# Attention and MLP on one core: the first k rows staged in the second x's place, its k bands copied by GpSimd, a new order of work

## The chip, the cores and the metric

The kernel runs on one core of a Trainium2 chip. The metric is the device time of one execution in microseconds (us); smaller is better. The engines work in parallel, each through its own list of instructions in a fixed order: TensorE (PE in the profile; its weight loads are PEld), VectorE (DVE), ScalarE (ACT), GpSimd (POOL) and SyncE (SP), which here issues all transfers between HBM and the on-chip memory SBUF. TensorE writes its results to PSUM.

## The reference

```python
# q, k, v: (4, 8, 768, 64) float32; w_in: (512, 2048); w_out: (2048, 512)
block, window = (32, 16)
k_sum = k.reshape(B, H, nb, block, D).max(axis=3)
v_sum = v.reshape(B, H, nb, block, D).mean(axis=3)
mask_l = np.abs(pos[:, None] - pos[None, :]) < window
scores_l = scale * np.matmul(q, k.transpose(0, 1, 3, 2))         # kept where mask_l
scores_s = scale * np.einsum('bhsd,bhnd->bhsn', q, k_sum) + np.log(block)
a = softmax(concatenate([where(mask_l, scores_l, -1e9), scores_s]))
attn = np.matmul(a, concatenate([v, v_sum], axis=2))
x = attn.transpose(0, 2, 1, 3).reshape(B * S, H * D)             # (3072, 512)
h = x @ w_in
out = np.maximum(0.01 * h, h) @ w_out
```

Each row attends to a band of 31 neighbours and to 24 block summaries (the maxima of k and the means of v over 32 rows), and an MLP with a leaky ReLU follows.

## The kernel before

The 3072 rows of x are worked on in 8 chunks of 384 rows, two for each batch. Attention makes x of a chunk, transposed, in 12 units: 4 pairs of heads (p) by 3 tiles of 128 rows. Per unit TensorE computes scores (`s`, L329), VectorE adds the mask and finds the extreme (L334), ScalarE takes the exponential (L341), VectorE normalises (L378 to L386), TensorE transposes the weights (`t`, L346), ScalarE copies them to SBUF (`pt`), TensorE multiplies them with v (`o`, L352), and x is stored as a high part (`xhi`, ScalarE) and the rest (`xlo`, VectorE), so that two reduced-precision matmuls and a third with the low half of the weights give nearly full precision.

The MLP of a chunk has 16 blocks f of 128 hidden columns. Per block twelve matmuls make `h` (L676: win_hi times x high, win_hi times x low, win_lo times x high, for 4 contraction parts); ScalarE makes `ghi` and `gs`, VectorE the low part `glo`; nine matmuls of 512 columns add to the outputs `a` (L695 to L697). The weights are loaded once and split into high and low halves by ScalarE and VectorE (L631 to L644) while chunks 0 and 1 run. The parts are: chunk 0 with blocks 0 to 9, all of chunk 1, chunk 0 with blocks 10 to 15, then chunk after chunk.

k comes as a window of 800 columns per pair of heads (`kn`); from it VectorE takes the maxima (`ksum`, L207), and ScalarE copies two bands of 3x96 columns per pair into the operand tile `k` that also holds q (L274); VectorE adds the maxima there (L289). The means of v of the first batch are made by six matmuls on TensorE (`vps`, L243, blocks `vb` of v), copied to SBUF by ScalarE (L248), and spread into the v tiles by GpSimd (L285).

The order of work is not written by hand. `Plan` gets every operation with an engine, an assumed cost, a priority and its needs, and lists them in the order in which they would run by these costs; the numbers at the head of the file (`PLACE`, `WS`, `XP`, `OFF`, `LOADS` and others) are priorities. Every engine then runs its list in that order. Where the plan leaves TensorE idle in the opening, matmuls on zeros (`spare`, L788) are put in. Buffers are rings: `big` has 6 buffers for k, v blocks and raw weights, `k` has 2, `v` 3, `pt` 2, `out` 3.

Of the kernel before, what the change touches and what calls it, by code (L numbers as in the profile page):

```python
# [23 lines left out]
LK = 120  # L24
# [25 lines left out]
KS = -4  # L50
XW = 1
B1 = 6
USQ = 1.424
WT = 1.15
# [92 lines left out]
def POOL(n):  # L147
    return 130 + 1.0 * n


def build(tc, ctx, a):
# [42 lines left out]
    def gate(b):  # L194
        return k_op[CPB * b - 1, 1] if b else []


    kn_op = {}

    def k_max(b, p, t, ahead):  # L200
        def load():
            x = new("big", ("kn", b * CPB, p), [128, 1024], bufs=BIG)
            nc.sync.dma_start(out=x[:, :S + 2 * WIN], in_=a["k"][b, p])

        def red():
            x = tl["kn", b * CPB, p][:, WIN:WIN + S].rearrange("p (n r) -> p n r", r=BLK)
            nc.vector.tensor_reduce(out=new("ksum", ("ksum", b, p), [128, NS], bufs=5), in_=x, axis=AX.X, op=ALU.max)  # L207
        key = ("kn", b * CPB, p)
        kn_op[key] = load_op(key, t - 1.3 - ahead, load, after=gate(b), alloc=[("big", key, BIG)], size=128 * (S + 2 * WIN) * 4)
        ksum_op[b, p] = P.op("DVE", DVE(S), t, red, after=[kn_op[key]], use=[key], alloc=[("ksum", ("ksum", b, p), 5)])  # L210
# [23 lines left out]
    def v_mean_pe(t):  # L234
        def load(j):
            x = new("big", ("vb", 0, j), [128, 1024], bufs=BIG)
            nc.sync.dma_start(out=x.rearrange("p (t d) -> p t d", t=2), in_=a["v0"][j])

        def mm(j, i):
            if i + j == 0:  # L240
                new("a1", ("vps",), [128, 512], src=ps_acc, bufs=1)
            n = 2 * j + i
            nc.tensor.matmul(tl["vps",][:NS], mask[:, 3 * LK + 20 - 4 * n:3 * LK + 44 - 4 * n], tl["vb", 0, j][:, 512 * i:512 * i + 512],  # L243
                             start=n == 0, stop=n == 5)

        def copy():
            tl["vsum", 0] = new("out", ("vs0",), [128, 512], bufs=TPC)[:NS]
            nc.scalar.copy(tl["vsum", 0], tl["vps",][:NS])  # L248
        prev = [mask_op]
        for j in range(3):  # L250
            o = load_op(("vb", 0, j), t - 4.5 + 0.1 * j, lambda j=j: load(j), alloc=[("big", ("vb", 0, j), BIG)], size=128 * 4096)
            for i in range(2):
                prev = [P.op("PE", 856, t, lambda i=i, j=j: mm(j, i), after=[o] + prev, use=[("vb", 0, j), ("vps",)],
                             alloc=[("a1", ("vps",), 1)] if i + j == 0 else [])]
        vsum_op[0] = P.op("ACT", ACT(512, True), t + 0.1, copy, after=prev, use=[("vps",)], alloc=[("out", ("vsum", 0), TPC)])


    def operands(c, p, t, ahead):
# [33 lines left out]
        if cb:  # L292
            kn_op[kw] = load_op(kw, t - 1.3 - ahead, load_k, alloc=[("big", kw, BIG)], size=128 * (T + 2 * WIN) * 4)
        ks = [P.op("ACT", ACT(TPC * 96), t - 0.6 + (0 if b else XW), lambda j=j: windows(j), after=[lq, kn_op[kw]], use=[kk, kw]) for j in range(2)]
        lv = load_op(("v", c, p), t - 0.6 - ahead, load_v, alloc=[("v", kv, VR)], size=96 * TPC * 1024)
# [63 lines left out]
    def unit(u):  # L359
# [59 lines left out]
        o = P.op("PE", 216, v + 1.2 + off("tr"), tr, after=[nm], use=[("e", m)], alloc=[("a0", kt, 1)])  # L419
        o = P.op("ACT", ACT(256, True), v + 1.3 + off("pt"), pt, after=[o] + pt_of.get(m, []), use=[kt, ("pt", m)] if u % 2 else [kt], alloc=[] if u % 2 else [("pt", ("pt", m), PTR)])  # L420
# [36 lines left out]
    def pair(m):  # L457
# [55 lines left out]
        al = [(f"x{XB[c]}", ("x", c), 1)] if r == 0 else []  # L513
        o1 = P.op("ACT", ACT(256, True), v2 + 0.3, xhi, after=[o] + ([x_op[c][0]] if r else []), use=[("s0", go), ("x", c)], alloc=al)
        o2 = P.op("DVE", DVE(256), v2 + 0.35 - XP, xlo, after=[o1], use=[("s0", go), ("x", c)])
# [28 lines left out]
    def quad(q):  # L544
# [16 lines left out]

        def xhi():
            nc.scalar.copy(x_of(xh, c, r, 512), tl["s0", kb1])
# [4 lines left out]
        o = burst(ka, pa, "s", 1280, qk, after=[y for x in ps for y in k_op[c, x]], use=kk)  # L568
        pts = []
        for m, kt, vt in ((ms[0], kb, pb), (ms[1], ka1, pa1)):  # L570
# [30 lines left out]
            nm = P.op("DVE", DVE(4 * LK), pa + 0.45 + d, nrm, after=[rc], use=[("e", m), ("z", m)])  # L601
            ot = burst(kt, vt, "t", 510, tr, after=[nm], use=[("e", m)])
            pts.append(P.op("ACT", ACT(512, True), vt + 0.2, pt, after=[ot], use=[("to", kt)], alloc=[("pt", ("pt", m), PTR)]))
        o = burst(kb1, pb1, "o", 1340, av, after=pts + [y for x in ps for y in v_op[c, x]], use=[("pt", m) for m in ms] + kv)
        al = [(f"x{XB[c]}", ("x", c), 1)] if r == 0 else []
        o1 = P.op("ACT", ACT(512, True), pb1 + 0.2, xhi, after=[o] + ([x_op[c][0]] if r else []), use=[("s0", kb1), ("x", c)], alloc=al)
        o2 = P.op("DVE", DVE(512), pb1 + 0.25 - XP, xlo, after=[o1], use=[("s0", kb1), ("x", c)])
# [234 lines left out]
```

## Time and profile before

| | before |
|---|---|
| device time, median of 3 runs | 641.48 us (640.58 to 642.33) |
| the profiled execution's own time | 640.98 us |
| its span, first to last instruction | 639.2 us |
| busy: PE, PEld | 633.7 us (99%), 557.6 us (87%) |
| busy: DVE, ACT, POOL | 263.4 us (41%), 293.2 us (46%), 4.4 us (1%) |
| mean granted TensorE clock | 0.999 |

All stretches are counted in us from the span's start. Busy time of TensorE is modelled from the starts of its pipelined matmuls, so two neighbouring rows can overlap a little; the distance between two starts tells what a step took.

### The profile page before, as it was taken

Reading aid. Unit: us, or ns where it says so; the run is one execution under the profiler, and the core shown is the slowest. Engines: PE = TensorE matmul, PEld = TensorE weight load, DVE = VectorE, ACT = ScalarE, POOL = GpSimd, SP = SyncE. Lnnn points to the kernel's source line nnn. Section 1 sums busy time; section 2 is a strip of 40 time slices with the busy share of each in tenths; the row PEclk is TensorE's granted clock in tenths of the full one; section 3 lists DMA queues with packets and bytes.
Section 4 is the critical chain, followed back from the end, with each engine's and each line's share of the span. In section 5 each row is a group of like instructions: output and inputs, shape, how many; then the busy total and the mean of one; then the engine's idle time right before and its main releaser. Section 6 shows DMA issues by size and latency. Waiting matters only on the chain.

```text
span 639.2 us, 11599 instructions
## 1 busy us (share of the span) xinstructions
PE 633.7 (99%) x4592; PEld 557.6 (87%) x4592; DVE 263.4 (41%) x881; ACT 293.2 (46%) x876; POOL 4.4 (1%) x10
## 2 busy tenths in 40 slices
PE   9999999999999999999999999999999999999997
PEld 7688888898888998888888888888898898989996
DVE  5899999512485213323533243132332422121111
ACT  5899985624655224435345254243543532222221
POOL 0200000000000000000000000000000000000000
PEclk9999999999999999999999999999999999999999
DMA  8897997200754100304332121111101200010001
GB/s 272 275 303 240 295 296 219 75 4 26 199 157 126 40 2 14 122 24 125 87 86 72 42 68 33 47 63 32 41 13 47 86 1 1 1 50 0 1 1 50
DMA packets 27206, 58.07 MB, mean 91 GB/s; under 512 B 3024, under 2 KB 13328, under 8 KB 27152
## 3 DMA queue, kind: packets, MB, share of 16 engines
q1 hardware_dynamic: 27152, 57.33, 29.3%
q8 instruction: 36, 0.59, 0.4%
q14 instruction: 18, 0.15, 0.1%
HBM read 48.97 MB, written 6.29 MB: 86 GB/s over the span
## 4 chain that ended last, share of the span: by engine, by line
PE 99%; ACT 0%; issue 0%; DVE 0%
PE h L676 42%; PE a L695 14%; PE a L697 14%; PE a L696 14%; PE spare L788 2%; PE vps L243 1%; PE t L346 1%; PE o L352 1%; PE s L329 1%; PE s_('B', 21)_5358 L352 0%; PE s_('B', 8)_2162 L352 0%; PE s_('B', 24)_6023 L352 0%; PE s_('B', 23)_5837 L352 0%; PE s_('B', 20)_5118 L352 0%; PE s_('B', 19)_4871 L352 0%; PE s_('B', 18)_4629 L352 0%
## 5 line engine op out<-in xcount | busy, mean ns | idle before, releaser
L676 PE MATMUL h<-x,win_hi 128*128 128x384 f32 x1024 | 262.8, 337 | 0.0
L686 DVE TENSOR_TENSOR glo<-gs,ghi 128x384 fp32r<-128x384 f32 x128 | 71.3, 557 | 304.5 <-ACT gs L680 304.2
L676 PEld LDWEIGHTS h<-x,win_hi 128*128 128x128 f32 x1024 | 185.8, 188 | 9.1 <-issue 0.2
L683 ACT ACTIVATE ghi<-h 128x384 fp32r<-128x384 f32 x128 | 62.8, 490 | 279.1 <-PE h L676 279.1
L676 PE MATMUL h<-x,win_lo 128*128 128x384 f32 x512 | 172.2, 336 | 0.0
L695 PE MATMUL a<-wout_hi,ghi 128*128 128x512 f32 x384 | 153.2, 399 | 0.0
L697 PE MATMUL a<-wout_hi,glo 128*128 128x512 f32 x384 | 151.1, 394 | 0.0
L696 PE MATMUL a<-wout_lo,ghi 128*128 128x512 f32 x384 | 150.2, 391 | 0.0
L676 PEld LDWEIGHTS h<-x,win_lo 128*128 128x128 f32 x512 | 96.1, 188 | 0.0
L697 PEld LDWEIGHTS a<-wout_hi,glo 128*128 128x128 f32 x384 | 72.1, 188 | 16.9 <-DVE glo L686 0.3
L696 PEld LDWEIGHTS a<-wout_lo,ghi 128*128 128x128 f32 x384 | 72.2, 188 | 11.3 <-DVE wout_lo L644 0.3
L695 PEld LDWEIGHTS a<-wout_hi,ghi 128*128 128x128 f32 x384 | 72.2, 188 | 10.5
L341 ACT ACTIVATE e<-e,m 128x120 f32<-128x120 f32 x192 | 73.4, 387 | 3.5 <-DVE m L334 3.5
L680 ACT ACTIVATE gs<-h 128x384 f32<-128x384 f32 x128 | 62.2, 486 | 0.0
L341 ACT ACTIVATION_READ_ACCUMULATOR e<-e,m 128x1 f32 x192 | 36.6, 191 | 0.0
L274 ACT COPY k<-kn 128x288 f32<-128x288 f32 x64 | 24.5, 432 | 5.9 <-DMA kn<-in_k_dram 5.9
L583 DVE TENSOR_TENSOR e<-e,z 128x480 f32<-128x480 f32 x36 | 23.6, 657 | 1.0
L638 DVE SCALAR_TENSOR_TENSOR raw<-raw 128x512 int32<-128x512 int32 x32 | 21.7, 689 | 0.7 <-ACT raw L635 0.3
L635 ACT ACTIVATE raw<-raw 128x512 f32<-128x512 f32 x32 | 21.4, 696 | 0.1
L207 DVE TENSOR_REDUCE ksum<-kn 128x24 f32<-128x768 f32 x16 | 15.1, 946 | 9.6 <-DMA kn<-in_k_dram 9.6
L334 DVE DVE_READ_ACCUMULATOR2_ANT m<- 128x1 f32 x192 | 15.9, 83 | 0.0
L223 DVE TENSOR_REDUCE vsum<-vb 96x32 f32<-96x1024 f32 x12 | 14.4, 1206 | 2.1 <-DMA vb<-in_vb_dram 2.1
(410 smaller groups left out, 455.8 us busy)
## 6 DMA issues: line engine op xcount, KB each, us to landing
raw<-in_w_dram SPq DMA_DIRECT2D x32, 512.0 KB
v<-in_v_dram SPq DMA_DIRECT2D x32, 288.0 KB
kn<-in_k_dram SPq DMA_DIRECT2D x16, 400.0 KB
k<-in_q_dram SPq DMA_DIRECT2D x32, 192.0 KB
out_dram<-out SPq DMA_DIRECT2D x21, 256.0 KB
vb<-in_vb_dram SPq DMA_DIRECT2D x12, 384.0 KB
kn<-in_k_dram SPq DMA_DIRECT2D x16, 208.0 KB
v<-vsum SPq DMA_DIRECT2D x24, 72.0 KB
```

Source lines behind the costliest of these rows:

```text
L274: nc.scalar.copy(k, x)
L341: nc.scalar.activation(out=e[:, n], in_=e[:, n], func=AF.Exp, scale=-1.0, bias=m[:, n:n + 1], accum_out=z[:, n:n + 1])
L583: nc.vector.tensor_tensor(out=e, in0=e, in1=z.unsqueeze(2).broadcast_to([128, 4, LK]), op=ALU.mult)
L635: nc.scalar.activation(out=hw(), in_=hw(), func=AF.Prelu, scale=2.0 ** -112, alpha=2.0 ** 32)
L638: nc.vector.scalar_tensor_tensor(out=li(), in0=hi_i(), scalar=3, in1=li(), op0=ALU.logical_shift_left, op1=ALU.bitwise_or)
L676: nc.tensor.matmul(h[:, :T], w[:, k, 128 * f:128 * f + 128], x[:, k], start=n == 0, stop=n == 11)
L680: nc.scalar.activation(out=new("gs", G("gs", f), [128, T], bufs=1), in_=tl[G("h", f)][:, :T], func=AF.Prelu, alpha=0.01)
L683: nc.scalar.activation(out=gnew("ghi", G("ghi", f)), in_=tl[G("h", f)][:, :T], func=AF.Prelu, alpha=0.01)
L686: nc.vector.tensor_tensor(out=gnew("glo", G("glo", f)), in0=tl[G("gs", f)], in1=tl[G("ghi", f)].bitcast(F32), op=ALU.subtract)
L695: nc.tensor.matmul(o, gh, wout_hi[:, f], start=f == f0, stop=False)
L696: nc.tensor.matmul(o, gh, wout_lo[:, f], start=False, stop=False)
L697: nc.tensor.matmul(o, gl, wout_hi[:, f], start=False, stop=f == f1 - 1)
```

## The change

The k windows of the first two head pairs go into two tiles of 128x1536 that take the place (the tag) of the second chunk's x, high and low; the tiles of that x are made when its first part is written, and its first write waits for the last readers of those k windows (`early_kn`). The `big` ring no longer holds them. The two k bands of each pair of chunk 0 are copied by GpSimd, not ScalarE. For chunk 0, every second tile of transposed weights (`pt`) comes from the `out` ring. The v means run in the order in which their blocks are loaded, and get a tile of their own. All tables of numbers and a few assumed costs are new, so the order of work is new on every engine.

```diff
-PLACE = {0: (0.0, 1.0), 1: (13.07, 0.61), 2: (22.42, 0.495), 3: (36.92, 0.51)}
+PLACE = {0: (0.0, 1.0), 1: (12.75, 0.61), 2: (22.42, 0.496), 3: (38.01, 0.639)}
...
-WS2 = 0.376
+WS2 = 0.302
...
-XP = 2.116
-VT = -1.915
+XP = 1.156
+VT = -1.316
...
-        x.append(cst.tile([128, NP, T], F32R, name=f"x{i}"))
+        x.append(cst.tile([128, NP, T], F32R, name=f"x{i}") if i % 2 == 0 else None)
+
+    def second(i, shape, dt, name):
+        return cst.tile(shape, dt, name=name, tag=f"x{2 * i + 1}", bufs=1)
...
     def k_max(b, p, t, ahead):
+        early = not b and p < 2
+
         def load():
-            x = new("big", ("kn", b * CPB, p), [128, 1024], bufs=BIG)
+            if early:
+                x = tl["kn", 0, p] = second(p, [128, NP * T], F32, f"kn_{p}")
+            else:
+                x = new("big", ("kn", b * CPB, p), [128, 1024], bufs=BIG)
...
             nc.tensor.matmul(tl["vps",][:NS], mask[:, 3 * LK + 20 - 4 * n:3 * LK + 44 - 4 * n], tl["vb", 0, j][:, 512 * i:512 * i + 512],
-                             start=n == 0, stop=n == 5)
+                             start=(j, i) == (js[0], 0), stop=(j, i) == (js[-1], 1))
...
-            tl["vsum", 0] = new("out", ("vs0",), [128, 512], bufs=TPC)[:NS]
+            tl["vsum", 0] = new("vs0", ("vs0",), [NS, 512], bufs=1)
...
-        for j in range(3):
+        js = sorted(range(3), key=lambda j: LOADS.index(("vb", 0, j)))
+        for j in js:
...
-            nc.scalar.copy(k, x)
+            nc.scalar.copy(k, x) if c else nc.gpsimd.tensor_copy(k, x)
...
+        if not c and p < 2:
+            early_kn.extend(ks + [ksum_op[b, p]])
...
-                new("pt", ("pt", m), [LK, 4, 128], bufs=PTR)
+                if m % 2:
+                    tl["pt", m] = new("out", ("pt", m), [128, 512], bufs=TPC).rearrange("p (h q) -> p h q", h=4)[:LK]
+                else:
+                    new("pt", ("pt", m), [LK, 4, 128], bufs=PTR)
...
         def xhi():
+            if c == 1 and r == 0:
+                xh[1], xl[1] = second(0, [128, NP, T], F32R, "xh1"), second(1, [128, NP, T], F32R, "xl1")
...
-        o1 = P.op("ACT", ACT(128, True), v + 2.0 + off("xhi"), xhi, after=[o] + ([x_op[c][0]] if r else []), use=[ko, ("x", c)], alloc=al)
+        o1 = P.op("ACT", ACT(128, True), v + 2.0 + off("xhi"), xhi, after=[o] + ([x_op[c][0]] if r else early_kn if c == 1 else []), use=[ko, ("x", c)], alloc=al)
```

On TensorE, in the opening, the v means (`vps<-vb_`, the block's number behind `vb_`) stood in blocks 0, 1, 2 with scores (`s_`, the unit's number) and transposes (`t_`) between them. Of before:

```order
L243 MATMUL vps<-vb_1_251,mask 24x512
L329 MATMUL s_8_373<-k_2_233 64x120 x2
L329 MATMUL s_8_374<-k_2_233 64x120 x2
L243 MATMUL vps<-vb_1_251,mask 24x512
L346 MATMUL t_391<-ident,e_304 120x128 x2
L243 MATMUL vps<-vb_2_109,mask 24x512 x2
```

Of the change, from the transpose ahead of block 2 to the scores behind the last mean:

```order
L358 MATMUL t_335<-ident,e_231 120x128 x2
L251 MATMUL vps<-vb_2_247,mask 24x512
L341 MATMUL s_7_349<-k_2_229 64x120 x2
L341 MATMUL s_7_350<-k_2_229 64x120 x2
L251 MATMUL vps<-vb_2_247,mask 24x512
L358 MATMUL t_365<-ident,e_302 120x128 x2
L251 MATMUL vps<-vb_1_253,mask 24x512
L358 MATMUL t_377<-ident,e_302 120x128 x2
L251 MATMUL vps<-vb_1_253,mask 24x512
L358 MATMUL t_387<-ident,e_341 120x128 x2
L341 MATMUL s_8_392<-k_2_229 64x120 x2
L341 MATMUL s_8_393<-k_2_229 64x120 x2
```

Block 2 now comes ahead of block 1, each of the six stands alone, and three transposes lie among them. Counted over the program, the `spare` matmuls are 63 ahead of the first scores and 97 behind them (20, 8, 4, 4, 13, 7, 3, 3, 9 and 26 between other work), where they were 61 and 103.

GpSimd's list, behind the making of the identity, held the four spreads of the v means; it now begins with the k bands (`k_` the operand tile of a pair, `kn_` its k window). Of the change:

```order
masks.py:199 AFFINE_SELECT ident<-ident 128x128
L283 COPY k_0_98<-kn_94 128x3x96 x2
L283 COPY k_1_96<-kn_100 128x3x96 x2
L283 COPY k_2_229<-kn_2_105 128x3x96 x2
L294 COPY v_0_271<-vs_390 24x768
L294 COPY v_1_289<-vs_390 24x768
L283 COPY k_3_298<-kn_3_279 128x3x96 x2
L294 COPY v_2_306<-vs_390 24x768
L294 COPY v_3_462<-vs_390 24x768
```

The bands of the last pair stand behind two of the spreads. On VectorE, at the end of the opening, the low half of w_in's block 1 (`win_lo<-raw_0_`) was made before the last two parts of the first x. Of before:

```order
L638 SCALAR_TENSOR_TENSOR raw_1_505<-raw_1_505 128x512
L644 TENSOR_TENSOR win_lo<-raw_0_493,win_hi 128x4x128
L406 TENSOR_TENSOR x_84<-o_650,x_80 128x128
L334 ISA e_684,m_685<-s_('g', 6, 1)_660,mask 128x120
L334 ISA m_685 128x1
L406 TENSOR_TENSOR x_84<-o_674,x_80 128x128
```

Of the change:

```order
L423 TENSOR_TENSOR x_83<-o_640,x_80 128x128
L497 TENSOR_TENSOR e_613<-e_613,z_615 128x480
L659 SCALAR_TENSOR_TENSOR raw_1_493<-raw_1_493 128x512
L423 TENSOR_TENSOR x_83<-o_665,x_80 128x128
L665 TENSOR_TENSOR win_lo<-raw_0_481,win_hi 128x4x128
L665 TENSOR_TENSOR wout_lo<-raw_1_493,wout_hi 128x512
L652 TENSOR_SCALAR raw_0_521<-raw_0_521 128x512
L652 TENSOR_SCALAR raw_1_506<-raw_1_506 128x512
```

The low half now follows the last part of x directly, and its companion in w_out follows it.

In the list of loads (`LOADS`) the q of pair 2 moves ahead of v's block 2, and the first weights and v tile move ahead of the last k window:

```diff
-... ('vb', 0, 0), ('kn', 0, 2), ('vb', 0, 2), ('q', 0, 2), ('vb', 0, 1), ('kn', 0, 3), ('w', 0, 0), ('v', 0, 0), ...
+... ('vb', 0, 0), ('kn', 0, 2), ('q', 0, 2), ('vb', 0, 2), ('vb', 0, 1), ('w', 0, 0), ('v', 0, 0), ('kn', 0, 3), ...
```

## Rows read from the trace of the kernel before

**Rows 1.** Stage, length, busy us (x) PE, PEld, DVE, ACT, POOL; clock, DMA, GB/s.

```profile
7.15:34.48 27.33, 27.17 (x358) 17.32 (x357) 22.39 (x113) 22.58 (x88) 3.66 (x4) 1.00 0.89 288
34.48:100.00 65.52, 65.49 (x480) 56.93 (x478) 63.97 (x175) 60.90 (x153) 0.00 (x0) 1.00 0.90 280
100.00:634.90 534.90, 534.88 (x3700) 477.29 (x3699) 175.67 (x592) 207.08 (x633) 0.00 (x0) 1.00 0.19 55
```

**Rows 2.** TensorE's waits, all of them.

```profile
PE spare L788 <- DVE zero L780: 1.0, 1, 1.0
```

**Rows 3.** TensorE in order of time, opening: start, us, engine, line, operation, count.

```profile
0.99 6.23 PE L788 MATMUL spare<-zero 128*128 128x128 bf16 x61 [0.99 <-DVE zero L780]
7.15 0.64 PE L329 MATMUL s<-k 64*64 64x120 f32 x16
7.72 1.40 PE L788 MATMUL spare<-zero 128*128 128x128 bf16 x22
...
9.62 1.04 PE L243 MATMUL vps<-vb,mask 128*24 128x512 f32 x2
10.59 0.44 PE L329 MATMUL s<-k 64*64 64x120 f32 x8
10.96 1.04 PE L243 MATMUL vps<-vb,mask 128*24 128x512 f32 x2
...
18.52 1.90 PE L243 MATMUL vps<-vb,mask 128*24 128x512 f32 x4
20.35 1.79 PE L788 MATMUL spare<-zero 128*128 128x128 bf16 x29
22.07 0.34 PE L352 MATMUL o<-pt,v 120*64 120x64 f32 x4
```

**Rows 4.** TensorE in order of time, two places.

```profile
38.09 0.40 PE L695 MATMUL a<-wout_hi,ghi 128*128 128x512 f32 x1
38.33 0.40 PE L696 MATMUL a<-wout_lo,ghi 128*128 128x512 f32 x1
...
54.56 0.48 PE L695 MATMUL a<-wout_hi,ghi 128*128 128x512 f32 x1
55.08 0.50 PE L696 MATMUL a<-wout_lo,ghi 128*128 128x512 f32 x1
```

**Rows 5.** ScalarE, VectorE and GpSimd in order of time; GpSimd's copies by their line.

```profile
3.81 0.76 ACT L274 COPY k<-kn 128x288 f32<-128x288 f32 x2 [1.79 <-DMA kn<-in_k_dram]
7.11 0.77 ACT L274 COPY k<-kn 128x288 f32<-128x288 f32 x2 [2.54 <-DMA kn<-in_k_dram]
L285 POOL COPY v<-vs x4: 814/855/1281, 21.1 to 23.9; 24x768 f32<-24x768 f32 x4
21.62 0.82 DVE L644 TENSOR_TENSOR win_lo<-raw,win_hi 128x512 fp32r<-128x512 f32 x1 [0.75 <-ACT win_hi L641]
```

**Rows 6.** SyncE's issues of transfers, opening.

```profile
0.74 0.38 SPq L203 DMA_DIRECT2D kn<-in_k_dram  x1
...
4.01 0.78 SPq L237 DMA_DIRECT2D vb<-in_v_dram  x1
9.62 0.33 SPq L269 DMA_DIRECT2D k<-in_q_dram  x1
```

**Rows 7.** VectorE and TensorE in order of time, end of the opening.

```profile
33.33 0.68 DVE L644 TENSOR_TENSOR win_lo<-raw,win_hi 128x512 fp32r<-128x512 f32 x1
34.33 0.29 DVE L406 TENSOR_TENSOR x<-o,x 128x128 fp32r<-128x128 f32 x1
34.48 0.63 PE L676 MATMUL h<-x,win_hi 128*128 128x384 f32 x2
35.48 0.33 PE L676 MATMUL h<-x,win_lo 128*128 128x384 f32 x1
```

**Rows 8.** The chain that ended last: a group of chunk 6, one of chunk 7.

```profile
511.40 2.09 PE h L676 x12
...
616.18 2.08 PE h L676 x12
```

More of the change, by code (lines that the diff above doesn't have):

```diff
@@ L44 @@
 WS = 0.721
-WS2 = 0.376
+WS2 = 0.302
 LD = 3.541
-XP = 2.116
-VT = -1.915
+XP = 1.156
+VT = -1.316
 KP = -1.757
-KS = -4
+KS = -3.674
 XW = 1
 B1 = 6
-USQ = 1.424
+USQ = 1.376
 WT = 1.15
@@ L208, in k_max @@
         key = ("kn", b * CPB, p)
-        kn_op[key] = load_op(key, t - 1.3 - ahead, load, after=gate(b), alloc=[("big", key, BIG)], size=128 * (S + 2 * WIN) * 4)
+        kn_op[key] = load_op(key, t - 1.3 - ahead, load, after=gate(b), alloc=[("early", key, 2) if early else ("big", key, BIG)], size=128 * (S + 2 * WIN) * 4)
         ksum_op[b, p] = P.op("DVE", DVE(S), t, red, after=[kn_op[key]], use=[key], alloc=[("ksum", ("ksum", b, p), 5)])
@@ L253, in v_mean_pe @@
                 prev = [P.op("PE", 856, t, lambda i=i, j=j: mm(j, i), after=[o] + prev, use=[("vb", 0, j), ("vps",)],
-                             alloc=[("a1", ("vps",), 1)] if i + j == 0 else [])]
-        vsum_op[0] = P.op("ACT", ACT(512, True), t + 0.1, copy, after=prev, use=[("vps",)], alloc=[("out", ("vsum", 0), TPC)])
+                             alloc=[("a1", ("vps",), 1)] if (j, i) == (js[0], 0) else [])]
+        vsum_op[0] = P.op("ACT", ACT(512, True), t + 0.1, copy, after=prev, use=[("vps",)], alloc=[("vs0", ("vsum", 0), 1)])
     def operands(c, p, t, ahead):
@@ L293, in operands @@
             kn_op[kw] = load_op(kw, t - 1.3 - ahead, load_k, alloc=[("big", kw, BIG)], size=128 * (T + 2 * WIN) * 4)
-        ks = [P.op("ACT", ACT(TPC * 96), t - 0.6 + (0 if b else XW), lambda j=j: windows(j), after=[lq, kn_op[kw]], use=[kk, kw]) for j in range(2)]
+        ks = [P.op("ACT" if c else "POOL", ACT(TPC * 96) if c else POOL(TPC * 96), t - 0.6 + (0 if b else XW), lambda j=j: windows(j),
+                   after=[lq, kn_op[kw]], use=[kk, kw]) for j in range(2)]
+        if not c and p < 2:
+            early_kn.extend(ks + [ksum_op[b, p]])
         lv = load_op(("v", c, p), t - 0.6 - ahead, load_v, alloc=[("v", kv, VR)], size=96 * TPC * 1024)
@@ L419, in unit @@
         o = P.op("PE", 216, v + 1.2 + off("tr"), tr, after=[nm], use=[("e", m)], alloc=[("a0", kt, 1)])
-        o = P.op("ACT", ACT(256, True), v + 1.3 + off("pt"), pt, after=[o] + pt_of.get(m, []), use=[kt, ("pt", m)] if u % 2 else [kt], alloc=[] if u % 2 else [("pt", ("pt", m), PTR)])
+        o = P.op("ACT", ACT(256, True), v + 1.3 + off("pt"), pt, after=[o] + pt_of.get(m, []), use=[kt, ("pt", m)] if u % 2 else [kt], alloc=[] if u % 2 else [("out", ("pt", m), TPC) if m % 2 else ("pt", ("pt", m), PTR)])
         pt_of.setdefault(m, [o])
@@ L493, in xhi @@
         def xhi():
+            if c == 1 and r == 0:
+                xh[1], xl[1] = second(0, [128, NP, T], F32R, "xh1"), second(1, [128, NP, T], F32R, "xl1")
             nc.scalar.copy(x_of(xh, c, r, 256), tl["s0", go][:, 256:])
@@ L513, in pair @@
         al = [(f"x{XB[c]}", ("x", c), 1)] if r == 0 else []
-        o1 = P.op("ACT", ACT(256, True), v2 + 0.3, xhi, after=[o] + ([x_op[c][0]] if r else []), use=[("s0", go), ("x", c)], alloc=al)
+        o1 = P.op("ACT", ACT(256, True), v2 + 0.3, xhi, after=[o] + ([x_op[c][0]] if r else early_kn if c == 1 else []), use=[("s0", go), ("x", c)], alloc=al)
         o2 = P.op("DVE", DVE(256), v2 + 0.35 - XP, xlo, after=[o1], use=[("s0", go), ("x", c)])
@@ L562, in xhi @@
         def xhi():
+            if c == 1 and r == 0:
+                xh[1], xl[1] = second(0, [128, NP, T], F32R, "xh1"), second(1, [128, NP, T], F32R, "xl1")
             nc.scalar.copy(x_of(xh, c, r, 512), tl["s0", kb1])
@@ L566, in xlo @@
             nc.vector.tensor_tensor(out=x_of(xl, c, r, 512), in0=tl["s0", kb1], in1=x_of(xh, c, r, 512).bitcast(F32), op=ALU.subtract)
-        o = burst(ka, pa, "s", 1280, qk, after=[y for x in ps for y in k_op[c, x]], use=kk)
+        o = burst(ka, pa, "s", 1090, qk, after=[y for x in ps for y in k_op[c, x]], use=kk)
         pts = []
@@ L601, in quad @@
             nm = P.op("DVE", DVE(4 * LK), pa + 0.45 + d, nrm, after=[rc], use=[("e", m), ("z", m)])
-            ot = burst(kt, vt, "t", 510, tr, after=[nm], use=[("e", m)])
+            ot = burst(kt, vt, "t", 470, tr, after=[nm], use=[("e", m)])
             pts.append(P.op("ACT", ACT(512, True), vt + 0.2, pt, after=[ot], use=[("to", kt)], alloc=[("pt", ("pt", m), PTR)]))
-        o = burst(kb1, pb1, "o", 1340, av, after=pts + [y for x in ps for y in v_op[c, x]], use=[("pt", m) for m in ms] + kv)
+        o = burst(kb1, pb1, "o", 1190, av, after=pts + [y for x in ps for y in v_op[c, x]], use=[("pt", m) for m in ms] + kv)
         al = [(f"x{XB[c]}", ("x", c), 1)] if r == 0 else []
-        o1 = P.op("ACT", ACT(512, True), pb1 + 0.2, xhi, after=[o] + ([x_op[c][0]] if r else []), use=[("s0", kb1), ("x", c)], alloc=al)
+        o1 = P.op("ACT", ACT(512, True), pb1 + 0.2, xhi, after=[o] + ([x_op[c][0]] if r else early_kn if c == 1 else []), use=[("s0", kb1), ("x", c)], alloc=al)
         o2 = P.op("DVE", DVE(512), pb1 + 0.25 - XP, xlo, after=[o1], use=[("s0", kb1), ("x", c)])
```

10 lines of the change are left out of this document (5 added, 5 removed).

## The prediction

> **What bounds the kernel now.** I read the stages first: from 7.15 us on TensorE is busy in all but a few hundredths of every stage, at a granted clock of 1.00, while VectorE and ScalarE are nearly full only until 100 us (63.97 and 60.90 of 65.52 us) and have room afterwards [rows 1]. The list of TensorE's own waits holds one entry, 1.0 us at the very start [rows 2]. A busy TensorE could still hide stretched matmuls, so I then read its rows in order of time. In the opening it runs its work back to back, with filler matmuls (L788, on zeros) where the order leaves room: 61 before the first scores, 22 behind them, 29 behind the v means [rows 3]; the kernel issues 164 in all. The clearest stretched step comes later: a 512-column matmul takes 0.24 us from start to start (38.09 to 38.33), but 0.52 us at 54.56 [rows 4].
>
> So the time is the length of TensorE's list. A change can gain only by taking fillers, waits or work from that list, and lose by adding waits. This bounds the gain: 0.3% of the time, about what a measurement of this kernel can tell from no change, is 1.9 us, and the list holds 103 fillers of 0.06 us behind the first scores (29 take 20.35 to 22.07, [rows 3]), about 6 us, that stand in for data not yet there.
>
> **Fillers and the list.** The order of the changed kernel has 63 fillers ahead of the first scores (+2) and 97 behind (-6): +0.12 - 0.36 = -0.24 us. The six v-mean matmuls stand apart now. One alone costs 0.97 us (9.62 to 10.59), two together 1.83 (18.52 to 20.35) [rows 3], so splitting that pair adds 2 x 0.97 - 1.83 = +0.11. All other matmuls are the same in number, and the attention bursts between the MLP's matmuls are entered as often as before (46 times). What moves among them (the first chunk's later products, chunk 3's attention) moves within a full list: nothing. Sum: -0.13 us.
>
> **Waits that go.** At 54.56 TensorE is held by the low half of w_out's block 3, and VectorE's order now makes that half before w_in's block 5 instead of behind it. I take back the 0.28 us of that row (0.52 - 0.24), with 0 and 0.5 as bounds, the latter if smaller stretches like it go too [rows 4].
>
> **Waits that come, one by one.**
>
> The k bands on GpSimd: eight copies of 128x288. No row has this form there. From below, 768 elements in 0.81 us [rows 5] scale to 0.31 us; from above, the whole 0.81. ScalarE's pairs take 0.76 to 0.77 [rows 5], so I take 0.4 each. Pair 0 can start when its k lands, 3.81, and is wanted at 7.26 (7.15 plus two fillers): hidden up to 1.7 us a copy. Pair 1 lands at 7.11 and is wanted at about 9.4 (7.26, scores 0.57, 20 fillers, half of the next scores): hidden up to 1.15 us a copy. Neither bound reaches TensorE. ScalarE loses eight copies, 3.0 us, but that frees TensorE of nothing, as it does not wait for ScalarE.
>
> The queue on SyncE: q of pair 2 is issued when a tile comes free, at 9.62 [rows 6]. The second block of v stood ahead of it (4.01); now it stands behind it, at about 10.0, and everything later stands behind that. The first k took from 0.74 to 3.81 from issue to use, 3.1 us for 400 KB, so 192 KB of q and 512 KB of v should be there by 13.5 to 14. TensorE's list wants the block at about 14.6: from the second scores' end at 9.6, two means, seven scores or transposes at 0.37 (10.59 to 10.96, [rows 3]) and 8 fillers. Hidden, with 0.6 us to spare; +0.5 as the upper bound. The two k tiles staged where the second x goes free two of the six staging buffers, so the loads behind it do not wait for buffers.
>
> The v means: by the new list the sixth matmul ends at about 19.6 (14.6, four means, three pieces of 0.37) instead of 20.35. From that end to the first product of weights and v there were 1.72 us in which ScalarE copied the means and GpSimd spread them (first copy from 21.1, 0.81 us) [rows 3, 5]. In the new list only three pieces of 0.37 and 8 fillers, 1.6 us, lie between: +0.1.
>
> The first weights: VectorE made the low half of w_in's block 1 at 33.33, ahead of the last x (34.33); now it comes behind it. That puts it at about 34.55 to 35.2 against its use at 35.48 [rows 7]: hidden, with some 0.3 us left. Behind it, VectorE's queue now holds 0.6 us more ahead of the first glo, whose use is also tight.
>
> For these together I take +0.25 us, from 0 to 1.0.
>
> GpSimd's copies also met VectorE once in this trace: beside them the subtraction L644 took 0.82 us, against 0.68 alone, and the copy beside it 1.28 instead of 0.81 [rows 5, 7]. The Trainium skill (SBUF — State Buffer, section "SBUF: two separate sides") states a harder rule: GpSimd and a VectorE instruction with two SBUF inputs take a shared port pair in turn, and each is held for the other's whole instruction. By the row the sum below stands; by the rule, with every hold on TensorE's path, it would be the 644.4 us of the second rival.
>
> **Sum.** -0.13 - 0.28 + 0.25 = -0.16 us on the profiled execution's 640.98 (its span is 639.2, with 1.78 around it): 640.8. The median of the runs, 641.48, lies 0.50 above the profiled execution, so 641.3; I say 641.2. By the bounds the work alone gives -0.6 to +0.9, and the three runs of before spread by 0.9 either way: 640.2 to 642.6 for this case.
>
> **Rivals.**
>
> *GpSimd holds TensorE (slower).* The eight copies and the four v copies share one queue in order. Pairs 1, 2 and 3 each have about 1.15 us a copy before TensorE waits; beyond it each pair costs 2 x (d - 1.15), so three cost 6 x (d - 1.15). At 1.28 us, the longest GpSimd copy in the trace, that is 0.8 us: still no measurable loss. It becomes one from d = 1.5 us; at 1.6 it is 2.7 us, 643.9. For it: the form was never seen here, and 128 partitions are more than 24. Against it: 0.81 us for 768 elements [rows 5]. Chance 0.08.
>
> *The shared port (slower).* Each of eight copies delays one of VectorE's normalisations, ahead of a transpose, by a whole copy: 8 x 0.4 = 3.2 us if all of it reached TensorE, 644.4; by the row's 0.14 it is 1.1 us, inside the bounds above. VectorE has 5 of 27 us free in the opening [rows 1], against it. Chance 0.04.
>
> *Moved tiles change the matmul's step (either side).* The x of odd chunks and tiles behind it lie elsewhere in memory. A twelve-matmul group takes 2.09 us, 174 ns a step. If a place changed the step by 2 ns, 1536 such matmuls would move by 3.1 us: 638.1 or 644.3. Against it: chunk 6 and chunk 7 read x from different tiles and show 2.09 and 2.08 [rows 8]. Chance 0.05 faster, 0.03 slower.
>
> *The change does what it says but there is nothing to win* is my forecast: ScalarE is relieved, loads have more room, and neither was what TensorE waited for. Chance 0.80.
>
> **The numbers.** Faster by over 0.3%: 0.05; within 0.3%: 0.80; slower: 0.08 + 0.04 + 0.03 = 0.15. The range takes the forecast's own, 640.2 to 642.6, and widens it for a faster execution of the day and for the nearer part of the slow cases: 639.8 to 643.1.
>
> **What would show it.** Right: no waits in TensorE's list beyond the start; the first scores at about 7.26, the last three matmuls of the first MLP group at 34.3 to 34.8 (34.48 before, [rows 7]); GpSimd's copies at 0.3 to 0.5 us; the stretch at 54.56 gone. Wrong: TensorE waiting for GpSimd before 25 us; copies above 1.15 us; a granted clock below 1.00 behind such a wait; or groups of twelve off 2.09 us. If TensorE's first scores came earlier than 7.2 us, my account of the fillers would be wrong.

## The result, and the profile after

The changed kernel is slower: median 644.37 us (643.81 to 644.57, 4 runs) against 641.03 us of the kernel before in the same session, ratio 1.005, 95% interval 1.0038 to 1.0062. That is 3.3 us more. I had forecast 641.2 us (639.8 to 643.1) and no change; the prediction was wrong. The profiled execution took 644.43 us with a span of 642.7, 3.5 more than that of before.

TensorE's waits in the changed kernel, the whole list ([rows 2] had one line); columns: us in total, times, longest:

```profile
PE o L364 <- DVE x L423: 1.2, 2, 0.9
PE spare L809 <- DVE zero L801: 1.0, 1, 1.0
PE s_('g', 13, 1)_1337 L364 <- DVE xl L516: 0.7, 1, 0.7
PE s L341 <- DVE m L346: 0.2, 1, 0.2
PE h L697 <- ACT win_hi L662: 0.2, 1, 0.2
```

TensorE of the changed kernel in order of time, from the first product of weights and v to the last three matmuls of the first MLP group, and four later places (start, us, engine, line, operation, count, wait in brackets):

```profile
6.49 0.64 PE L341 MATMUL s<-k 64*64 64x120 f32 x16
...
21.64 0.69 PE L364 MATMUL o<-pt,v 120*64 120x64 f32 x16
22.26 0.90 PE L809 MATMUL spare<-zero 128*128 128x128 bf16 x13
24.02 0.45 PE L364 MATMUL o<-pt,v 120*64 120x64 f32 x8 [0.86 <-DVE x L423]
...
26.02 0.45 PE L364 MATMUL o<-pt,v 120*64 120x64 f32 x8 [0.31 <-DVE x L423]
...
34.98 1.62 PE L809 MATMUL spare<-zero 128*128 128x128 bf16 x26
36.42 0.60 PE L697 MATMUL h<-x,win_hi 128*128 128x384 f32 x2
...
64.11 0.65 PE L358 MATMUL to_('g', 10, 1)_1072<-ident,e 128*120 128x128 f32 x4
64.98 0.62 PE L697 MATMUL h<-x,win_hi 128*128 128x384 f32 x2 [0.22 <-ACT win_hi L662]
...
65.99 0.51 PE L697 MATMUL h<-x,win_hi 128*128 128x384 f32 x2
...
83.87 0.51 PE L364 MATMUL s_('g', 13, 1)_1337<-pt,v 120*64 120x64 f32 x10 [0.69 <-DVE xl L516]
...
95.02 0.34 PE L697 MATMUL h<-xh,win_hi 128*128 128x384 f32 x1
...
638.38 0.39 PE L718 MATMUL a<-wout_hi,glo 128*128 128x512 f32 x1
```

The same places of before, where [rows 3, 7] do not show them: the last fillers, the group at block 6, block 2 of chunk 1, the last matmul.

```profile
33.72 0.95 PE L788 MATMUL spare<-zero 128*128 128x128 bf16 x14
...
62.48 0.66 PE L346 MATMUL to_('g', 10, 1)_1077<-ident,e 128*120 128x128 f32 x4
...
63.51 0.51 PE L676 MATMUL h<-x,win_hi 128*128 128x384 f32 x2
...
91.75 0.51 PE L676 MATMUL h<-x,win_hi 128*128 128x384 f32 x2
...
634.48 0.40 PE L697 MATMUL a<-wout_hi,glo 128*128 128x512 f32 x1
```

Set beside the same matmuls of before, the list falls behind in steps:

| the same matmul in both traces | before | after | behind |
|---|---|---|---|
| first scores | 7.15 | 6.49 | -0.66 |
| first product of weights and v | 22.07 | 21.64 | -0.43 |
| last three of the first MLP group begin | 34.48 | 36.42 | +1.94 |
| chunk 0, block 7 | 67.14 | 69.62 | +2.48 |
| chunk 1, block 2 | 91.75 | 95.02 | +3.27 |
| the last matmul | 634.48 | 638.38 | +3.90 |

So 2.4 us are lost between the first product and the first MLP group, 1.3 up to block 2 of chunk 1, and 0.6 in small steps over the remaining 543 us, without a wait: 4.3 in all, from 0.4 ahead to 3.9 behind. In the first of these stretches stand 61 fillers (13, 7, 3, 3, 9 and 26), where before had 33.

What stood in front of the late pieces: VectorE and GpSimd at 21 to 26 us, then ScalarE and VectorE ahead of the last x of chunk 0, then VectorE at 83 us:

```profile
21.58 1.32 DVE L665 TENSOR_TENSOR win_lo<-raw,win_hi 128x512 fp32r<-128x512 f32 x1 [0.23 <-ACT win_hi L662]
22.83 0.94 DVE L215 TENSOR_REDUCE ksum<-kn 128x24 f32<-128x768 f32 x1
23.69 0.47 DVE L423 TENSOR_TENSOR x<-o,x 128x128 fp32r<-128x128 f32 x2
24.92 0.86 DVE L298 COPY k<-ksum 128x144 f32<-128x144 f32 x1
20.77 1.59 POOL L294 COPY v<-vs 24x768 f32<-24x768 f32 x2 [9.72 <-ACT vs L256]
22.31 1.25 POOL L283 COPY k<-kn 128x288 f32<-128x288 f32 x2
...
34.60 0.69 ACT L656 ACTIVATE raw<-raw 128x512 f32<-128x512 f32 x1
35.19 0.65 ACT L662 CAST win_hi<-raw 128x512 fp32r<-128x512 f32 x1
35.74 0.27 ACT L420 CAST x<-o 128x128 fp32r<-128x128 f32 x1
35.52 0.69 DVE L659 SCALAR_TENSOR_TENSOR raw<-raw 128x512 int32<-128x512 int32 x1
36.12 0.28 DVE L423 TENSOR_TENSOR x<-o,x 128x128 fp32r<-128x128 f32 x1
...
82.80 0.68 DVE L665 TENSOR_TENSOR win_lo<-raw,win_hi 128x512 fp32r<-128x512 f32 x1
83.40 0.42 DVE L516 TENSOR_TENSOR xl<-s_('g', 12, 1)_1293,xh 128x256 fp32r<-128x256 f32 x1
```

The reader is to see two things. Low parts of x (L423, L516) come behind work that TensorE does not yet want: the maxima of pair 3 at 22.83, weights at 34.6 to 35.5 and at 82.8. And L665 takes 1.32 us beside GpSimd's copies, where it takes 0.68 elsewhere; the copy L298 takes 0.86 instead of 0.23 ([rows 7] have 0.68 for the first; before's L289 took 0.23). The 26 fillers up to 36.42 hide a wait: the last x is done only then, 1.4 us after its product ended (0.8 in before).

### The profile page after: what moved, and what is told of

Its sections match the earlier page's. It is cut to its first block, busy times and chain, and to the rows that moved or that the text cites. A ratio compares the mean times of both kernels' runs of the same rounds, so it can differ in the third digit from the quotient of the medians.

```text
span 642.7 us, 11604 instructions
## 1 busy us (share of the span) xinstructions
PE 635.1 (99%) x4588; PEld 556.6 (87%) x4588; DVE 266.0 (41%) x881; ACT 292.0 (45%) x868; POOL 7.7 (1%) x18
## 4 chain that ended last, share of the span: by engine, by line
PE 89%; ACT 5%; DVE 4%; DMA 1%; issue 1%; SPq 0%; DVEq 0%
PE h L697 39%; PE a L716 13%; PE a L718 13%; PE a L717 13%; ACT e L353 1%; PE vps L251 1%; DVE raw L659 1%; ACT raw L656 1%; DMA kn<-in_k_dram 1%; ACT win_hi L662 1%; DVE win_lo L665 1%; ACT wout_hi L662 0%; PE t L358 0%; DVE glo L707 0%; ACT ghi L704 0%
## 5 line engine op out<-in xcount | busy, mean ns | idle before, releaser
L697 PE MATMUL h<-x,win_hi 128*128 128x384 f32 x512 | 131.2, 337 | 0.2 <-ACT win_hi L662 0.2
L697 PEld LDWEIGHTS h<-x,win_hi 128*128 128x128 f32 x512 | 93.0, 188 | 5.0 <-ACT win_hi L662 0.5
L697 PE MATMUL h<-xh,win_hi 128*128 128x384 f32 x256 | 86.6, 338 | 0.0
L697 PE MATMUL h<-x,win_lo 128*128 128x384 f32 x256 | 86.4, 338 | 0.1
L697 PE MATMUL h<-xl,win_hi 128*128 128x384 f32 x256 | 86.0, 336 | 0.0
L697 PE MATMUL h<-xh,win_lo 128*128 128x384 f32 x256 | 85.9, 336 | 0.0
L697 PEld LDWEIGHTS h<-xh,win_hi 128*128 128x128 f32 x256 | 48.1, 188 | 2.6 <-issue 0.2
L697 PEld LDWEIGHTS h<-xl,win_hi 128*128 128x128 f32 x256 | 48.1, 188 | 2.3
L697 PEld LDWEIGHTS h<-x,win_lo 128*128 128x128 f32 x256 | 48.0, 188 | 0.4 <-DVE win_lo L665 0.4
L697 PEld LDWEIGHTS h<-xh,win_lo 128*128 128x128 f32 x256 | 48.1, 188 | 0.0
```

## The experiments

All times are medians, with the ratio to the kernel before on the same chip. "In place" means that every engine's list stays as it was but for what is named; `todo` is the plan's finished list, and `ahead` and `behind` move one operation in it. "Replanned" means that the plan made all lists anew.

**GpSimd.** *kbands_scalar*, the changed kernel:

```diff
-            nc.scalar.copy(k, x) if c else nc.gpsimd.tensor_copy(k, x)
+            nc.scalar.copy(k, x)
```

> The changed kernel with every instruction list as it is, but the eight k-band copies of chunk 0 done by ScalarE at the same places of the order (pair 3's behind the third xhi, where ScalarE waited 1.63 us). Theory 1, GpSimd's copies hold VectorE: the copy L298 at 24.9 us falls from 0.86 to about 0.23 us, the subtraction L665 at 21.6 us stays between 0.8 and 1.32 us (the v copies still run beside it), TensorE's two waits for xlo (1.2 us) fall to 0.5 us or less, and the time to 643.4-643.9 us, against 644.4 of the changed kernel. Theory 2, only the order counts (the ksum of pair 3 ahead of xlo): the waits stay within 0.2 us and the time is 644.2-644.7. Theory 3, ScalarE's 3 us were needed: above 644.7.

Measured 643.98 us, ratio 1.0044 (1.0032 to 1.0056), whose interval overlaps the changed kernel's. VectorE in order of time, and TensorE's wait for it:

```profile
21.04 1.29 DVE L665 TENSOR_TENSOR win_lo<-raw,win_hi 128x512 fp32r<-128x512 f32 x1 [0.25 <-ACT win_hi L662]
24.23 0.85 DVE L298 COPY k<-ksum 128x144 f32<-128x144 f32 x1
```

```profile
PE o L364 <- DVE x L423: 1.0, 2, 0.9
```

The k bands are gone from GpSimd and VectorE is held as before: the v copies, which the old kernel has too, are enough. The time lies between the ranges of theories 1 and 2; the rows decide, and theory 1 falls for the k bands.

*before_gpsimd*, the kernel before, with the bands of chunk 0 on GpSimd in place (the reverse of that diff):

> The kernel before, every list in its old order, with the eight k-band copies of chunk 0 done by GpSimd. Theory 1: VectorE's instructions beside these copies (L289, L406, L644 at 21 to 25 us) grow by 0.3 to 0.6 us each where they meet, TensorE gets waits for x in the opening, and the time is 641.4-642.3 (against 641.0-641.5). Theory 2: no wait, no change, within 0.3 us of the kernel before. If ScalarE's relief were a gain, it would show here: 640.5 or less.

Measured 641.39 us, ratio 1.0001 (0.9992 to 1.001). VectorE was held even longer than in the changed kernel, and TensorE waited for the x behind it (VectorE, then TensorE, in order of time):

```profile
21.70 1.52 DVE L644 TENSOR_TENSOR win_lo<-raw,win_hi 128x512 fp32r<-128x512 f32 x1 [0.74 <-ACT win_hi L641]
23.47 0.45 PE L352 MATMUL o<-pt,v 120*64 120x64 f32 x8 [0.28 <-DVE x L406]
```

The profiled execution took 643.2 us, the longest of the eleven. Besides this wait it has others, of 0.5 us for `pt` and of 0.6 and 0.5 us for weights at 50 us; that the bands caused those is not shown. Over the eleven executions no loss can be told.

*kbands3_first*, the changed kernel, in place: `ahead(todo, k_op[0, 3][j], v_op[0, 0][1])` for both bands j.

> The changed kernel with GpSimd's two k-band copies of pair 3 (22.31-23.5 us) moved ahead of its first v copy, into the time before 20.7 us in which GpSimd is idle. Theory 1: the copy L298 at 24.9 no longer runs beside a GpSimd copy and falls from 0.86 to about 0.23 us, the wait of 0.31 us at 26.0 goes, and the time is 643.7-644.1; the subtraction L665 stays near 1.3 us, since v copies still run beside it. Theory 2: L298 falls, but the wait of 0.86 us behind the ksum stays and the time is 644.2-644.7. If GpSimd's lateness itself counted, TensorE's next scores would move, and no more than 0.2 us.

Measured 645.65 us (644.06 to 651.0), ratio 1.0082. My premise was wrong: GpSimd's time before 20.7 us was idle, but pair 3's data were not there. GpSimd waits, the v copies stand behind it, and TensorE waits for them (GpSimd in order of time, and the list of waits):

```profile
22.46 0.80 POOL L283 COPY k<-kn 128x288 f32<-128x288 f32 x2 [11.31 <-DMA kn<-in_k_dram]
```

```profile
PE o L364 <- POOL v L294: 2.3, 1, 2.3
```

**Mending single places of the new order.** All on the changed kernel, in place. *ksum3_later*: `behind(todo, ksum_op[0, 3], x_op[0][3])`.

> The changed kernel with one instruction moved: VectorE takes the maxima of pair 3 (L215, 0.94 us at 22.83) behind the first two xlo instead of ahead of them. Theory 2, the order makes the wait: xlo starts at about 22.9 instead of 23.69, TensorE's wait of 0.86 us at 24.0 falls to 0.1 or less, and 0.8 us of it reach the end: 643.4-643.8 us. Rival, the wait is given back later (the weights or the second wait of 0.31 us at 26.0 come due instead): the wait goes, and the time stays at 644.1-644.6. If GpSimd alone were at fault (theory 1 with nothing left for the order), the xlo would be stretched or late where it now stands, and the wait would stay above 0.5.

Measured 643.97 us, ratio 1.0043 (1.0031 to 1.0055). The wait for x went, and another came, since the scores of pair 3 need what now comes later:

```profile
PE t L358 <- DVE k L298: 1.0, 1, 1.0
```

*weights_late*:

```diff
-    todo = P.order()
+    todo = P.order(); ahead(todo, w_op[6, 0][0], w_op[5, 1][0]); ahead(todo, w_op[6, 0][1], w_op[5, 1][1]); ahead(todo, x_op[1][8], w_op[10, 0][0]); behind(todo, x_op[1][9], x_op[1][8])
```

> The changed kernel with two places of its order mended: block 6's w_in halves ahead of block 5's w_out halves on ScalarE and VectorE (they held TensorE 0.47 and 0.27 us at 64.5 and 65.3), and x of unit (12,1), high on ScalarE and low on VectorE, ahead of the weights of block 10 (the wait of 0.7 us at 83.1). Theory 2, each late piece in the new order is paid in full, since TensorE's list is otherwise full: both go, 1.3 to 1.4 us less, 642.9-643.3 against 644.4. Rival, each is given back by the next late piece behind it: 643.9-644.5.

Measured 643.81 us, ratio 1.0055 (1.0038 to 1.0073). The wait at 83 us is gone; at block 6 the low half is late in place of the high one (0.5 us). Against the changed kernel's median that is 0.6 of the hoped 1.3; two of its six executions took over 646 us.

*last_x_first*: `ahead(todo, x_op[0][22], w_op[1, 0][0])`, the low part ahead of L659, and 12 fillers fewer.

> The changed kernel with the last x of chunk 0 ahead of the weights that stand before it (high part ahead of win_hi of block 1 on ScalarE, low part ahead of the L659 on VectorE), and 12 of the 26 fillers before the first group's last three matmuls left out. If x held the group: those three start 0.6-0.7 us earlier, 643.7 against 644.4; if the weights of block 1, now 0.3 us later, hold the next group instead, half of it is given back, 644.0-644.1. If the fillers' stretch stood for something else, an open wait of 0.6 us takes their place and nothing changes: 644.3.

Measured 644.16 us, ratio 1.0049 (1.0037 to 1.0062). In the trace the group comes 0.7 us nearer to the first product, and the block-3 group stands again where it stood.

*three_mended*, the three together:

> The changed kernel with three mends together: the ksum of pair 3 behind the first xlo (alone -0.4), block 6's weights and the x of unit (12,1) earlier (alone -0.5), and the last x of chunk 0 ahead of the weights (the run beside this one). If late pieces are paid one by one, their gains add: 642.8-643.2. If each only uncovers the next late piece, the three together give no more than the best of them: 643.7-644.0.

Measured 643.79 us, ratio 1.0045 (1.0032 to 1.0057): no better than the best of them. In the traces each mend uncovers another late piece.

*few_fillers*: `begun = o.get("mlp", False) or o["at"] > 22000`.

> The changed kernel without the 61 filler matmuls (spare, L809) that stand behind the first product of weights and v (13, 7, 3, 3, 9, 26); the kernel before has 33 there. If they only stand in for data that is not there, TensorE waits openly for the same time: 644.0-644.7, with new waits of about 2.5 us in all between 22 and 36.4 us and the last three matmuls of the first MLP group at the same place relative to the first product. If they hold TensorE themselves, the part of their 3.5 us that nothing else needs goes: 28 more of them than before at 0.058 us are 1.6 us, so 642.6-643.5. If the idle time lowers the granted clock, the time rises above 645.

Measured 648.14 us, ratio 1.0108 (1.0093 to 1.0122). The waits that the fillers had covered stand open, and the granted clock falls; the list of waits, and the windows with the columns of [rows 1]:

```profile
PE o L364 <- DVE x L423: 2.2, 2, 1.7
PE h L697 <- ACT x L420: 1.0, 1, 1.0
```

```profile
22.00:45.00 23.00, 18.97 (x165) 14.89 (x162) 17.50 (x65) 15.70 (x56) 3.22 (x5) 0.70 0.81 240
45.00:60.00 15.00, 15.00 (x145) 12.73 (x144) 13.56 (x44) 12.90 (x38) 0.00 (x0) 1.00 0.76 255
```

*chunk1_later*: chunk 1's first scores and their work behind the last x of chunk 0, 19 fillers fewer.

> The changed kernel with chunk 1's first scores (group 6,1: its k bands and four exponentials on ScalarE, its masks and norm on VectorE, its scores on TensorE) moved behind the last x of chunk 0 and behind the first group's last three matmuls, and 19 of the fillers there left out. If this work in front of the last units is what makes x late: the last three matmuls of the first group start at about 35.0 instead of 36.4 us, and 0.6 to 1.3 us reach the end: 643.1-643.8. If the list behind it gives it back (the same work, the weights of block 1): 644.1-644.6.

Measured 648.45 us, ratio 1.0113 (1.0099 to 1.0128). The clock fell here too (0.63 from 26 to 40 us of the profiled execution), so it does not answer its question.

**Parts, numbers and load order apart.** *before_parts*, the kernel before with the staging, the `pt` tiles, the sums' tile and the GpSimd bands of the diff, in place:

> All parts of the change except the means' order (the first k rows in the second x's place, the odd pt from the out ring, the v sums in a tile of their own, the k bands by GpSimd) in the kernel before, with every engine's list in the old order. If the loss lies in the new order alone: 640.8-641.8, like the kernel before and like the run with GpSimd alone. If the parts cost by themselves (tiles in other places, buffers of the out ring shared, GpSimd): 643 or more, and the place of the first new wait names the part. If the place of x in memory changed the matmul's step, groups of twelve in odd chunks would leave 2.08-2.09 us.

Measured 641.76 us, ratio 1.0011 (1.0002 to 1.002). Most of it is in the length of TensorE's own steps. The same two matmuls as in the table, block 2 of chunk 1 and the last one, here:

```profile
92.21 0.34 PE L691 MATMUL h<-xh,win_hi 128*128 128x384 f32 x1
...
635.61 0.39 PE L712 MATMUL a<-wout_hi,glo 128*128 128x512 f32 x1
```

From the first to the second it is 543.4 us, where before takes 542.7, and this run's list has no wait in between. The trace of every run that has the parts shows 543.4 there, whichever its order (the changed kernel 95.02 to 638.38, *after_old_tables* too); that of every run without them shows 542.7, *before_gpsimd* and *before_xp* among them. So these 0.6 us come with the parts that move or share tiles, not from the order and not from GpSimd. Added up over this stretch, the 116 groups of nine products into `a` take 1.3 us more than in before and the 116 groups of twelve 0.6 us less; which of these parts does it is not shown.

*before_loads*, the kernel before with the new `LOADS` on SyncE's queue alone, in place:

> The kernel before with nothing changed but the order of the first twenty transfers on SyncE's queue, which is that of the changed kernel (q of pair 2 ahead of block 2 of v, the first raw weights and the first v ahead of the k of pair 3); all other lists are old. Theory 3, the later landings cost (block 2 of v 14.4 instead of 11.4 us, k of pair 3 19.9 instead of 16.4): the list behind them moves by 0.5 to 2 us, 641.6-643. Rival, hidden as I had predicted: 640.8-641.4.

Measured 648.18 us, ratio 1.0111 (1.0095 to 1.0126). In the old order the maxima of pair 3 stand early (18.10 us in before, without a wait); with the k of pair 3 behind the first weights and v, VectorE stands still for it, TensorE for VectorE, and the clock falls (VectorE in order of time, the wait, the window):

```profile
21.01 0.95 DVE L207 TENSOR_REDUCE ksum<-kn 128x24 f32<-128x768 f32 x1 [3.03 <-DMA kn<-in_k_dram]
```

```profile
PE o L352 <- DVE x L406: 3.6, 1, 3.6
```

```profile
22.00:36.00 14.00, 10.45 (x117) 7.28 (x117) 9.36 (x42) 7.89 (x31) 2.38 (x3) 0.63 0.66 200
```

*after_loads*, the changed kernel with the old `LOADS` on SyncE's queue alone, in place, and *after_loads_replan*, with the old `LOADS` replanned:

> The changed kernel with only SyncE's first twenty transfers in the old order (block 2 of v ahead of q of pair 2, k of pair 3 ahead of the first weights and the first v); every other list as changed. If a transfer that comes late holds a list directly: waits go and the time is 643.4 or less. If the load order works only through the lists that were made to fit it (the ksum of pair 3 put late because its k lands late): nothing waits for these transfers now, 644.0-644.7.

> The same old load order in the changed kernel, but the plan makes all lists anew from it, with the other new numbers. If the load order is the cause: the scores of pair 3 and the first MLP group come 1 us or more earlier and the time is 642.5 or less. If any list made from numbers that were not fitted to it loses a few us: 643.5 or more.

Measured 644.29 us, ratio 1.006 (1.0042 to 1.0077), with the changed kernel's waits; and 645.64 us, ratio 1.0074 (1.0062 to 1.0086). The load order binds the lists to it, but putting it back gains nothing.

*after_old_tables* and *before_new_tables*, both replanned:

> The changed kernel's parts (k rows in the second x's place, bands by GpSimd, pt from the out ring, means in load order) with all tables of numbers and assumed costs of the kernel before; the plan makes its own order from them. If the new numbers are what costs (theory 2): 640.8-642.2. If the parts are what costs, whatever the order: 643.8-645.

> The kernel before with the changed kernel's tables of numbers and assumed costs, none of its other parts. If the new numbers cost by themselves: 643.5-645. If they cost only with the parts: 640.8-642.2. As the numbers were not made for these parts, a larger loss (645 and more) would say only that numbers and parts belong together.

Measured 645.28 us, ratio 1.0067 (1.0055 to 1.0079), and 642.74 us, ratio 1.0024 (1.0016 to 1.0033). The old numbers make a slow order with the new parts, above both forecasts; the new numbers cost with the old parts, less than forecast. *before_numbers*, the latter with the old `LOADS`:

> The kernel before with all new numbers and costs but the old load order; beside the run with the new load order too (642.7). If the load order is what costs there: 640.8-641.5. If the other numbers cost: 642.3 or more.

Measured 642.92 us, ratio 1.003 (1.0018 to 1.0041): the other numbers cost, with either load order.

**One number.** *before_xp* and *xp_old*, both replanned:

```diff
-XP = 2.116
+XP = 1.156
```

> The kernel before with one new number alone: XP (how far ahead VectorE takes the low part of x) 1.156 instead of 2.116; the plan makes new lists, with 59 fillers behind the first product of weights and v instead of 33, 40 of them ahead of the first group's last three matmuls instead of 14. If a list made from one number that the others were not fitted to loses by its own late x: 26 fillers at 0.058 us are 1.5 us, 642.3-643.5. If the number is harmless and the plan's fillers stand for nothing: 640.8-641.4.

> The changed kernel with the old XP (2.116) alone; the plan makes new lists, with 63 fillers behind the first product instead of 61. If the late low part of x (the waits at 24, 26 and 83 us) comes from this number: 643.4 or less. If the other numbers and the parts set the lists and this one is small: 643.9-645.

Measured 642.7 us, ratio 1.0029 (1.0018 to 1.004), inside the forecast of the fillers; and 644.22 us, ratio 1.0057 (1.0043 to 1.007), so putting XP back alone does not mend the changed kernel. Of the first, VectorE and TensorE in order of time, and a line of its waits:

```profile
34.60 0.69 DVE L644 TENSOR_TENSOR wout_lo<-raw,wout_hi 128x512 fp32r<-128x512 f32 x1
35.21 0.28 DVE L406 TENSOR_TENSOR x<-o,x 128x128 fp32r<-128x128 f32 x1
33.56 2.41 PE L788 MATMUL spare<-zero 128*128 128x128 bf16 x40
35.78 0.60 PE L676 MATMUL h<-x,win_hi 128*128 128x384 f32 x2
```

```profile
PE s_('g', 13, 1)_1372 L352 <- DVE x L497: 0.9, 1, 0.9
```

A smaller XP gives VectorE's low part of x a later place: behind wout_lo at 34.60, where before it was done at 34.62 [rows 7]; 40 fillers stand where there were 14, the group starts 1.3 us later, and the low part at 83 us is late by 0.9 (0.7 in the changed kernel).

## Why the prediction was wrong

**The fillers were counted over the whole list.** I took two fillers more ahead of the first scores and six fewer behind them as a gain of 0.24 us. Where they stand decides. Of the 97, 36 stand ahead of the first product (before: 70) and 61 behind it (before: 33). The 34 that went ahead of it freed little: the product came 0.43 us earlier, not the 2.0 of 34 x 0.058. The 28 that came behind it stand ahead of all the rest: 26 take 1.44 us (34.98 to 36.42), so 28 take 1.55. They stand where the plan expects data late, and the data are late: with all 61 left out, TensorE waits openly instead (*few_fillers*), and with 12 left out and the last x earlier, the group comes 0.7 us sooner (*last_x_first*). In *before_xp*, with 26 more fillers, the group comes 1.64 us later behind the first product than in before (14.05 us after 12.41), near the 1.5 of the fillers; of its 1.8 us in the end, the wait at 83 us is a part.

**"What moves among them moves within a full list: nothing."** This is the sentence that failed. TensorE's matmuls move at no cost only if VectorE and ScalarE, which I had read as nearly full until 100 us [rows 1], still make x and the weights in time. In the new lists they don't, at four places: 1.2 us at 24 and 26; 0.85 at block 6, of which 0.2 is an open wait (from the transposes to the fourth matmul 1.88 us, 64.11 to 65.99, in place of 1.03, 62.48 to 63.51); 0.7 at 83. That is 2.7 us in place of the 0.25 (0 to 1.0) which I had put on waits, and none of it is at the places that I had named (k bands, block 2 of v, v means, win_lo of block 1). My bounds came from the pieces I had looked at; the low part of x, whose number XP stood in the diff, was not among them.

**Right in mechanism.** GpSimd's bands take 0.40 us each for pairs 0 to 2 (0.80 for two) and 1.25 for the two of pair 3, and TensorE waits for none of them. The stretch at 54.56 went for the most part: the step there is 0.32 us (56.45 to 56.77) after 0.52. The v means end at 20.03 (forecast 19.6, before 20.35). Most groups of twelve take 2.08 to 2.10 us (2.08 and 2.09 before, [rows 8]). The clock stayed at 1.00.

**The first scores** came at 6.49, against 7.26 forecast, with two fillers more; I had written that this would mean a wrong account of the fillers. In other traces with before's list ahead of them they came at 5.9 to 7.3, so the pace of the first fillers differs between executions, and this early lead is gone by the v means (9.69 after 9.62).

**The rivals.** *The shared port* touched the path, though not as I had priced it. VectorE is held for more than the 0.14 us that I took from the row: L665 is 0.64 us longer (1.32 for 0.68), L298 0.63. The rule that I had quoted from the Trainium skill (SBUF — State Buffer, section "SBUF: two separate sides"), that a GpSimd instruction holds such a VectorE instruction for its whole length, is nearer to the 0.64 than my 0.14. These two stand just ahead of the low parts of x for which TensorE waits at 24 and 26. By the rows, without the first hold the wait of 0.86 us would be about 0.2, and without the second that of 0.31 would be gone (estimates). The k bands are not needed for this, since the v copies hold as long alone (*kbands_scalar*); and an order with x ahead of the maxima has no wait for x although L665 takes 1.32 us there too (*ksum3_later*). No run takes the v copies off GpSimd, so how the 1.2 us divide between the order and the port is open. That the rival's time, 644.4, is the measured one is a coincidence: its eight bands of 0.4 us are not what happened. *Moved tiles* happened in small: not on the twelve products with x, where I looked, but mostly on the nine behind them, 0.6 us in all in place of 3.1 (*before_parts*). I had put nothing on it in the sum. *GpSimd holds TensorE* did not happen.

**What is shown and what is open.** Shown: the parts cost 0.1% with the old lists (*before_parts*, all but the means' order), 0.6 us of it in TensorE's steps whatever the order; and every list that the plan made from inputs other than before's is slower, by 0.24 to 0.74%. One number, XP, gives as much on the old parts as all the new numbers do (1.0029; 1.0024 and 1.003). Open: which input makes the rest of the 3.3 us in the changed kernel, where XP put back gains nothing that can be told, and the port's share in it. No version that I ran beats the kernel before.

## What to carry to other kernels

A change of a planner's numbers is a new program: read the first places at which the busy engine's inputs come later, not the sum of its instructions, and look at VectorE's and ScalarE's lists in front of these inputs. Fillers hide waits, so a list without waits is not a list without slack: count them ahead of and behind the point from which transfers no longer set the pace. To tell a change's parts from the order that it leads to, run the parts with the old lists; here that took one kernel and separated 0.1% from 0.5%. Then compare the distance between two late matmuls in both traces: it shows a change of step too small to see in one instruction.

## What the runs showed of the hardware

In two runs open waits of TensorE in the opening cost more than their length. In the changed kernel, waits of 0.86 and 0.31 us left the granted clock at 1.00. Where one wait was 1.7 us, with two of 0.4 to 0.5 soon after (*few_fillers*), or 3.6 us (*before_loads*), the mean granted clock was 0.70 from 22 to 45 us and 0.63 from 22 to 36 us, between its two levels of 1.2 and 2.4 GHz, before it was 1.00 again; the first was 3.8 us slower than the changed kernel that it came from, the second 7.3 us slower than the kernel before. The product of eight matmuls, 0.38 us from start to start at full clock, took 0.61 to 0.63 there. With the fillers left in, the changed kernel kept its clock over the same late data in all four executions. It is not certain: *weights_late* and *after_loads* have the same waits of 0.9 and 0.3 us, and three of their twelve executions had a mean clock of 0.991 to 0.994 and took 646.35 to 648.01 us; of *kbands3_first*, with a wait of 2.3 us in the profiled execution, three took 644.1 to 644.3 at 1.00 and three 647.0 to 651.0 at 0.989 to 0.997.

VectorE's subtraction of 128x512 (`win_lo`) took 0.68 us alone and 0.82 (before), 1.29 (*kbands_scalar*), 1.32 (the change) and 1.52 us (*before_gpsimd*) beside GpSimd's copies; its copy of 128x144 took 0.23 alone and 0.85 and 0.86 beside them.
